# Running block sums of gate and up: kept in one PSUM bank instead of added on VectorE

## The chip, the cores and the metric

The kernel runs on one core of one Trainium2 chip. The metric is the device time of one execution in microseconds (us), of which a median over runs is given. TensorE (PE in the profile) multiplies, with its weight loads listed as PEld; VectorE (DVE), ScalarE (ACT) and GpSimd (POOL) work element by element; SyncE (SP) issues DMAs. Each engine runs its own instructions in order. Products land in PSUM, which has eight banks of 128 x 512 fp32 here; everything else lies in SBUF.

## The reference, cut to what matters

```python
xn = _layernorm(x)                      # x: 2048 x 512
s  = _A_ref(xn, wqkv, w_phi, wo)        # linear attention, 32 heads of 16
gate = xn @ W_gate                      # 512 x 1376
up   = xn @ W_up
h    = gate * (gate > 0) * up           # relu(gate) * up
g    = silu(h @ W_down)                 # 1376 x 512
return x + s * g
```

## The kernel before

**Precision.** Every matmul operand is split into a high part and a remainder, both fp32r. One product is then three matmuls (low x high, high x low, high x high), written by `mm3`; with two tiles of the contraction that is six matmuls of 128 x 128 by 128 x 512. `split` makes the two parts: ScalarE copies the high one (`hh`), GpSimd subtracts for the low one (`hl`).

**Stages.** First come the projections of k, v and q for 16 tiles of 128 tokens, whose state products gather in four PSUM banks, the list `PKV`. Then come two halves. Each handles two blocks of 512 tokens: the gate/up stage over `NF` = 11 blocks of 128 columns of F (f = 0 to 10), with the down-projection of earlier blocks woven in, and then a tail with the rest of the down-projection, the SiLU and the output. The first half also splits all weights for the first time (`f_prep`); the split weights are spilled to memory and reloaded (`f_reload`) later.

**Gate/up by seven products.** For one f, two token blocks times two halves of the contraction, for gate and for up, would be eight block products; seven are formed instead, in the manner of Strassen and Winograd: the inputs A11, A12, A22 and the sums S1 to S4 lie ready in `XT`, and sums of the weights in wa, wb, wc, wd. In `gate_up` (lines 535 to 588) the products are, by the names used below:

| name | bank | input, weight | then, before the change |
|---|---|---|---|
| P1 | pa | A11, wa | ScalarE copies it to t1 (`t<-pa`) |
| P2 | pb | S2, wb | VectorE: m = pb + t1 (`u<-pb,t`) |
| P3 | pc | S3, wb | e7 = pc + m on VectorE (`e<-pc,u`); where `copied`, ScalarE copies pc (`e<-pc`) |
| P4 | pd | S1, wc | VectorE: e7 = pd + e7 (`e<-pd,e`) |
| P5 | pc, onto P3 | A22, wc | VectorE: pc = pc + m (`pc<-pc,u`); where `copied`, GpSimd before it: e7 = e7 + m (`e<-e,u`) |
| P6 | pa, onto P1 | A12, wa | VectorE: e7 = max(pc, 0) * e7, then the split of h1 |
| P7 | pd, onto P4 | S4, wd | VectorE: m = pd + m (`u<-pd,u`), m = max(pa, 0) * m (`u<-pa,u`), the split of h0 put off to the next block (`LATE`, `last_split`) |

`copied` holds in the second half from f = 2. In the profile a tile's name stands without its number, so m is `u`, t1 is `t` and e7 is `e`.

**What else runs meanwhile.** `run` steps `gate_up` from yield to yield. After the third, fifth, sixth and seventh yield it takes one step of the down-projection (`down`, bank `py`) if one is pending; each step covers two blocks of F. Steps become pending after f = 1, 3, 5 and 7, eight at a time, and first read h1 of those two blocks. The sums of the steps are VectorE additions in the first half (`y<-py,y`), and ScalarE copies with GpSimd additions in the second. In between, `pace.pump()` lets a planner, `Clock`, add work of other chains: the queries' softmax (`q_pair`, mostly VectorE), their products (`pnum`), and the weight splits. The planner keeps an estimated time for each engine and adds work only while an engine's estimated backlog is below a limit (`LIMIT`). All instructions stay in program order on their engine.

At f = 10 the pending steps have been drained and the queries finished before `gate_up` begins. In the first half, `used(c)` there reloads input c for the second half as soon as its last product is issued; `halfway` reloads the later weights of f + 1.

Of the kernel before, what the change touches and what calls it, by code (L numbers as in the profile page):

```python
# [8 lines left out]
F32R = mybir.dt.float32r  # L9
AF = mybir.ActivationFunctionType  # L10
ALU = mybir.AluOpType
AX = mybir.AxisListType

P = 128
# [6 lines left out]
NF = -(-F // P)  # L21
BT = 512
TPB = BT // P
NB = S // BT
NG = 8
# [10 lines left out]
A11, A12, A22, S1, S2, S3, S4 = range(7)  # L36
# [112 lines left out]
def layer_kernel(ctx: ExitStack, tc: tile.TileContext, x, wkT, wqT, wv, wo, wf, cst, out):  # L149
# [6 lines left out]
    def ps(shape=(P, 512), name="ps"):  # L156
        return pp.tile(list(shape), F32, tag="ps", name=name)
# [7 lines left out]
    def u2(shape, name, dt=F32):  # L165
        return sb.tile(list(shape), dt, tag="u2", bufs=B2, name=name)
# [10 lines left out]
    def add(engine, o, a, b, op=ALU.add):  # L177
        engine.tensor_tensor(o, a, b, op=op)
# [4 lines left out]
    def split(hi, lo, src, lo_engine=None):  # L183

        nc.scalar.activation(hi, src, AF.Copy)
        add(lo_engine or nc.vector, lo, src, f32(hi), ALU.subtract)

    def mm3(ps_out, w, m, ks, first=True, last=True):

        n = len(ks)  # L190
        for i, k in enumerate(ks):
            (wh, wl), (mh, ml) = w(k), m(k)
            mm(ps_out, wl, mh, first and i == 0, False)
            mm(ps_out, wh, ml, False, False)
            mm(ps_out, wh, mh, False, last and i == n - 1)
            if i < n - 1:
                pace.pump()
# [222 lines left out]
    def kv_products(n):  # L420
        phl, vhl = PHI.pop(n), VH.pop(n)
        if n == 0:
            PKV.extend(ps((P, 2, 256), name="pkv") for _ in range(NG // 2))
        for g in range(NG):
            mm(PKV[g // 2][:, g % 2, :], vhl[:, g, :, :], phl[:, g, :, :],
               n == 0 and g % 2 == 0, n == N - 1 and g % 2 == 1)
# [88 lines left out]
    def f_reload(f, part):  # L515
        if part == 0:
            FT[f] = [w_pair("wa"), w_pair("wb"), None, None]
            for i, t in enumerate([*FT[f][0], *FT[f][1]]):
                nc.sync.dma_start(f32(flat3(t)), wspill[f][i])
            return  # L520
        FT[f][2:] = w_pair("wc"), u2((P, 2, 2, P), "wd", F32R)
        WD[f] = u2((P, D), "fdh", F32R), u2((P, D), "fdl", F32R)
        for i, t in enumerate([*FT[f][2], FT[f][3], *WD[f]]):
            nc.sync.dma_start(f32(flat3(t)), wspill[f][4 + i])

    def w_of(f, i, c=None):
        t = FT[f][i]
        if c is None:
            return lambda k: (t[:, 0, k, :], t[:, 1, k, :])
        return lambda k: (t[0][:, c, k, :], t[1][:, c, k, :])  # L530

    def a_of(c):
        return lambda k: (XT[:, c, 0, k, :], XT[:, c, 1, k, :])

    def gate_up(f, copied, used, halfway):

        pa = ps(name="pa")
        mm3(pa, w_of(f, 0, 0), a_of(A11), range(2))
        used(A11)
        t1 = u2((P, BT), "t1")  # L540
        nc.scalar.activation(t1, pa, AF.Copy)
        last_split()
        yield
        pb = ps(name="pb")
        mm3(pb, w_of(f, 1, 0), a_of(S2), range(2))
        used(S2)
        m = u2((P, BT), "u2")
        add(nc.vector, m, pb, t1)
        yield
        pc = ps(name="pc")  # L550
        mm3(pc, w_of(f, 1, 1), a_of(S3), range(2))
        FT[f][1] = None
        used(S3)
        halfway()
        e7 = u2((P, BT), "e7")
        if copied:
            nc.scalar.activation(e7, pc, AF.Copy)
        else:
            add(nc.vector, e7, pc, m)
        yield  # L560
        pd = ps(name="pd")
        mm3(pd, w_of(f, 2, 0), a_of(S1), range(2))
        used(S1)
        add(nc.vector, e7, pd, e7)
        yield
        mm3(pc, w_of(f, 2, 1), a_of(A22), range(2), first=False)
        FT[f][2] = None
        used(A22)
        if copied:
            add(nc.gpsimd, e7, e7, m)  # L570
        add(nc.vector, pc, pc, m)
        yield
        mm3(pa, w_of(f, 0, 1), a_of(A12), range(2), first=False)
        FT[f][0] = None
        used(A12)
        h1 = u2((P, BT), "hh", F32R), u2((P, BT), "hl", F32R)
        nc.vector.scalar_tensor_tensor(e7, pc, 0.0, e7, op0=ALU.max, op1=ALU.mult)
        split(*h1, e7, nc.gpsimd)
        yield
        mm3(pd, w_of(f, 3), a_of(S4), range(2), first=False)  # L580
        used(S4)
        add(nc.vector, m, pd, m)
        nc.vector.scalar_tensor_tensor(m, pa, 0.0, m, op0=ALU.max, op1=ALU.mult)
        h0 = u2((P, BT), "hh", F32R), u2((P, BT), "hl", F32R)
        LATE.append(lambda: split(*h0, m, nc.gpsimd))
        FT.pop(f)
        HS[f] = [h0, h1]
        yield

    HS, Y, LATE = {}, {}, []  # L590

    def last_split():
        while LATE:
            LATE.pop()()
# [465 lines left out]
    def run(g, per=1):  # L1060
        n = 0
        for _ in g:
            pace.pump()
            n += 1
            if pending and n in (3, 5, 6, 7):
                if next(pending[0], pending) is pending:
                    pending.pop(0)
                    if pending:
                        next(pending[0])
                pace.pump()  # L1070
# [7 lines left out]
    for half in range(2):  # L1078
        b0, b1 = 2 * half, 2 * half + 1
        for f in range(NF):  # L1080
            if half == 0:
                at[0] = N + f
                pace.finish(preps, lambda: f in DONE)
                if f == 0:
                    queries = pace.add(all_queries(0), 20)
            if half == 1 and f == 0:
                queries = pace.add(all_queries(1), 5)
            again = f + 1 < NF and (half or f + 1 in AHEAD)
            if again and f + 1 not in FT:
                f_reload(f + 1, 0)  # L1090
            if f == NF - 1:
                drain()
                pace.finish(queries)
                for q in QUERIES[half][:4]:
                    if q not in OF:
                        o_load(q)
                WO = wo_load()
            if f == NF - 2 and not half:
                for q in QUERIES[half][:2]:
                    o_load(q)  # L1100

            def used(c):
                if half == 0 and f == NF - 1:
                    nc.sync.dma_start(f32(XT[:, c]), xt_spill[:, c])
            run(gate_up(f, half and f > 1, used, lambda: again and f_reload(f + 1, 1)))
            for c, fs in enumerate(CHUNKS[:-1]):
                if f == fs[-1]:
                    pending.extend(down((b0, b1)[j], j, fs, c == 0) for j in (1, 0))

        last_split()  # L1110
        drain()
        if half == 0:
            f_reload(0, 0)
            f_reload(0, 1)
        fs = CHUNKS[-1]
        for j, b in enumerate((b1, b0)):
            j = 1 - j
            if b == b0:
                for q in QUERIES[half][:2]:
                    o_split(q)  # L1120
            parts = {}
            for i in range(TPB):
                if j == 1 and i < 3:
                    parts[i] = ps(name="py")
                    down_rows(parts[i], i, j, fs[:-1], True, False)
            for i in range(TPB):
                if i in parts:
                    down_rows(parts[i], i, j, fs[-1:], False, True)
                else:
                    parts[i] = ps(name="py")  # L1130
                    down_rows(parts[i], i, j, fs, True, True)
                y_sum(b, i, parts[i], False, True)
                y = Y[b][:, i, :]
                nc.scalar.activation(y, y, AF.Silu)
                if b * TPB + i in yspill:
                    pace.when(y, lambda t=b * TPB + i, y=y: nc.sync.dma_start(yspill[t], y))
                pace.pump()
        for g in fs:
            HS.pop(g), WD.pop(g)
        qs = QUERIES[half]  # L1140
        for m, q in enumerate(qs):
            if half == 0 and m == 1:
                f_reload(1, 0)
            if m + 2 < len(qs):
                o_split(qs[m + 2])
            if m + 4 < len(qs):
                o_load(qs[m + 4])
            for j in range(2):
                out_tile(2 * q + j, WO)
                pace.pump()  # L1150
# [56 lines left out]
```

## Time and profile before

| | |
|---|---|
| median of 3 runs | 580.02 us (577.81 to 581.3) |
| span of the profiled execution | 576.0 us |
| own device time of that execution | not listed; the median is 4.0 us above the span |
| TensorE busy | 565.9 us, 98% |
| VectorE, ScalarE, GpSimd busy | 409.0, 280.8, 417.1 us |
| granted TensorE clock | 1.000 |
| first half, f = 0 to 10 | from 175.9 us on |
| second half, f = 0 to 10 | from 368.4 us on |

Rows of the timeline read: start, duration, engine, line, operation, output<-inputs, shapes and count. Matmuls are pipelined, so the recorded durations of neighbours overlap and the spacing of their starts is what counts. A wait row reads: engine and tile, what released it, total us, number, longest. In a group row the count is followed by the busy us and the mean ns of one, and after the second bar by the idle time before them.

### The profile page before, as it was taken

Reading aid. Unit: us, or ns where it says so; the run is one execution under the profiler, and the core shown is the slowest. Engines: PE = TensorE matmul, PEld = TensorE weight load, DVE = VectorE, ACT = ScalarE, POOL = GpSimd, SP = SyncE. Lnnn points to the kernel's source line nnn. Section 1 sums busy time; section 2 is a strip of 40 time slices with the busy share of each in tenths; the row PEclk is TensorE's granted clock in tenths of the full one; section 3 lists DMA queues with packets and bytes.
Section 4 is the critical chain, followed back from the end, with each engine's and each line's share of the span. In section 5 each row is a group of like instructions: output and inputs, shape, how many; then the busy total and the mean of one; then the engine's idle time right before and its main releaser. Section 6 shows DMA issues by size and latency. Waiting matters only on the chain.

```text
span 576.0 us, 8601 instructions
## 1 busy us (share of the span) xinstructions
PE 565.9 (98%) x2848; PEld 479.1 (83%) x2848; DVE 409.0 (71%) x609; ACT 280.8 (49%) x505; POOL 417.1 (72%) x351
## 2 busy tenths in 40 slices
PE   8899999999999999999999999999999999999997
PEld 7788888989898788888888888788888888888886
DVE  3798666768674989699888442599896969874322
ACT  3796876756544536526435133223545444534600
POOL 0669888977879177999798424364759888888475
PEclk9999999999999999999999999999999999999999
DMA  8248899884589927878877999998656766659963
GB/s 315 91 151 225 225 289 273 248 231 95 150 229 283 382 77 262 268 259 273 279 266 259 254 298 424 392 371 302 168 198 201 236 204 191 204 157 318 256 188 111
DMA packets 82523, 138.25 MB, mean 240 GB/s; under 512 B 7600, under 2 KB 30512, under 8 KB 81584
## 3 DMA queue, kind: packets, MB, share of 16 engines
q1 hardware_dynamic: 79024, 125.60, 64.9%
q0 software_dynamic: 3312, 12.06, 11.0%
q8 instruction: 22, 0.36, 0.3%
q14 instruction: 21, 0.17, 0.1%
q10 hardware_dynamic: 144, 0.07, 0.0%
HBM read 77.14 MB, written 52.69 MB: 225 GB/s over the span
## 4 chain that ended last, share of the span: by engine, by line
PE 49%; DVE 2%; POOL 1%; issue 0%; ACT 0%; POOLq 0%; DVEq 0%
PE py L52 16%; PE pso L52 8%; PE pa L52 7%; PE pc L52 7%; PE pd L52 7%; PE pb L52 3%; PE pnum L52 2%; POOL y L52 0%; DVE mx L52 0%; POOL pTl L52 0%; DVE eq L52 0%; DVE e L52 0%; POOL hl L52 0%; DVE pq L52 0%; POOL ez L52 0%
## 5 line engine op out<-in xcount | busy, mean ns | idle before, releaser
L52 PE MATMUL py<-fdh,hl 128*128 128x512 f32 x176 | 68.6, 390 | 0.0
L52 PE MATMUL py<-fdh,hh 128*128 128x512 f32 x176 | 68.5, 389 | 0.0
L52 PE MATMUL py<-fdl,hh 128*128 128x512 f32 x176 | 68.5, 389 | 0.0
L52 PE MATMUL pa<-XT,wa 128*128 128x512 f32 x264 | 67.3, 390 | 0.0
L52 POOL TENSOR_TENSOR hl<-e,hh 128x512 fp32r<-128x512 f32 x22 | 29.1, 1322 | 40.6 <-ACT hh L52 35.7
L52 PEld LDWEIGHTS pa<-XT,wa 128*128 128x128 f32 x264 | 49.3, 188 | 10.1
L52 POOL TENSOR_TENSOR phl<-ek,phl 128x1024 fp32r<-128x1024 f32 x15 | 36.4, 2426 | 24.5 <-ACT phl L52 24.5
L52 ACT ACTIVATE hh<-e 128x512 fp32r<-128x512 f32 x22 | 13.9, 633 | 72.7 <-DVE e L52 67.9
L52 DVE TENSOR_TENSOR y<-py,y 128x512 f32<-128x512 f32 x40 | 27.5, 688 | 29.0 <-PE py L52 29.0
L52 POOL TENSOR_TENSOR hl<-u,hh 128x512 fp32r<-128x512 f32 x22 | 28.6, 1298 | 18.7 <-ACT hh L52 18.5
L52 PEld LDWEIGHTS py<-fdh,hh 128*128 128x128 f32 x176 | 33.0, 188 | 7.0
L52 PEld LDWEIGHTS py<-fdl,hh 128*128 128x128 f32 x176 | 33.1, 188 | 6.9
L52 PEld LDWEIGHTS py<-fdh,hl 128*128 128x128 f32 x176 | 33.0, 188 | 6.8
L52 POOL TENSOR_TENSOR ez<-eq,zB 128x1024 f32<-128x1024 f32 x16 | 38.7, 2426 | 0.0
L52 PE MATMUL pc<-XT,wc 128*128 128x512 f32 x132 | 35.2, 393 | 0.3 <-DVE e L52 0.3
L52 PE MATMUL pq<-XT,wqh 128*128 128x256 f32 x192 | 35.4, 282 | 0.0
L52 POOL TENSOR_TENSOR ol<-of,oh 128x1024 fp32r<-128x1024 f32 x8 | 19.1, 2402 | 21.7 <-ACT oh L52 10.5
L52 PE MATMUL pv<-wvh,XT 128*128 128x512 f32 x96 | 33.2, 400 | 1.0 <-ACT pqs L52 1.0
L52 PE MATMUL pd<-XT,wd 128*128 128x512 f32 x132 | 34.1, 392 | 0.0
L52 PE MATMUL pc<-XT,wb 128*128 128x512 f32 x132 | 33.7, 389 | 0.0
L52 PE MATMUL pd<-XT,wc 128*128 128x512 f32 x132 | 33.7, 389 | 0.0
L52 PE MATMUL pb<-XT,wb 128*128 128x512 f32 x132 | 33.5, 389 | 0.0
(166 smaller groups left out, 1665.6 us busy)
## 6 DMA issues: line engine op xcount, KB each, us to landing
zacc<-ek POOLq DMA_DIRECT2D x15, 512.0 KB, 5.7
xts<-XT SPq DMA_DIRECT2D x4, 1792.0 KB
XT<-xts SPq DMA_DIRECT2D x7, 1024.0 KB, 18.8
wa<-ws SPq DMA_DIRECT2D x26, 256.0 KB, 4.8
wb<-ws SPq DMA_DIRECT2D x26, 256.0 KB, 4.8
wc<-ws SPq DMA_DIRECT2D x26, 256.0 KB, 5.4
rawg<-wf SPq DMA_DIRECT2D x22, 256.0 KB, 3.9
ws<-wa SPq DMA_DIRECT2D x22, 256.0 KB, 4.2
```

Of the source, the lines that this page charges most:

```text
L52: return self.tc.keep_in_program_order(op(*a, **k))
```

## The change

For f = 1 to 10 of both halves the running sums stay in one PSUM bank for the whole stage. It is the fourth bank of `PKV`, named `pseed` now, whose state products have been read by then; it is never given back, so seven banks are left for all other tiles. ScalarE copies P1 into it, and P2, P3 and P5 accumulate onto that copy; ScalarE copies the bank out after P2 (m) and after P3 (e7). The products run in the order P1, P7 of the block before, P2, P6, P3, P4, P5. P7 and what follows it are put off into the next block (`CARRY`, `last_product`), and the split of h1 is put off too (`LATE`). f = 0 keeps its old form in `gate_up_apart`, up to the split of h1 and P7, which are put off as well. Steps of the down-projection still follow the yields 3, 5, 6 and 7, which are now those after P2, P3, P4 and P5. `halfway` is now called after P6.

```diff
@@ kv_products
-            PKV.extend(ps((P, 2, 256), name="pkv") for _ in range(NG // 2))
+            PKV.extend(ps((P, 2, 256), name=s) for s in ("pkv", "pkv", "pkv", "pseed"))
@@ gate_up
-    def gate_up(f, copied, used, halfway):
+    def gate_up(f, used, halfway):
         pa = ps(name="pa")
         mm3(pa, w_of(f, 0, 0), a_of(A11), range(2))
         used(A11)
+        if f == 0:
+            yield from gate_up_apart(f, pa, halfway)
+            return
+        pb = PKV[-1].rearrange("p a f -> p (a f)")
+        nc.scalar.activation(pb, pa, AF.Copy)
+        last_split()
+        yield
+        last_product()
+        yield
+        last_split()
+        mm3(pb, w_of(f, 1, 0), a_of(S2), range(2), first=False)
+        used(S2)
+        m = u2((P, BT), "u2")
+        nc.scalar.activation(m, pb, AF.Copy)
+        yield
+        mm3(pa, w_of(f, 0, 1), a_of(A12), range(2), first=False)
+        FT[f][0] = None
+        used(A12)
+        halfway()
+        yield
+        mm3(pb, w_of(f, 1, 1), a_of(S3), range(2), first=False)
+        FT[f][1] = None
+        used(S3)
+        e7 = u2((P, BT), "e7")
+        nc.scalar.activation(e7, pb, AF.Copy)
+        yield
+        pd = ps(name="pd")
+        mm3(pd, w_of(f, 2, 0), a_of(S1), range(2))
+        used(S1)
+        add(nc.vector, e7, pd, e7)
+        yield
+        mm3(pb, w_of(f, 2, 1), a_of(A22), range(2), first=False)
+        FT[f][2] = None
+        used(A22)
+        finish_f(f, pa, pb, pd, m, e7, used)
+        yield
+
+    def gate_up_apart(f, pa, halfway):
...
-        if copied:
-            nc.scalar.activation(e7, pc, AF.Copy)
-        else:
-            add(nc.vector, e7, pc, m)
+        add(nc.vector, e7, pc, m)
...
-        if copied:
-            add(nc.gpsimd, e7, e7, m)
         add(nc.vector, pc, pc, m)
         yield
         mm3(pa, w_of(f, 0, 1), a_of(A12), range(2), first=False)
         FT[f][0] = None
-        used(A12)
+        finish_f(f, pa, pc, pd, m, e7, lambda c: None)
+        yield
+
+    CARRY = []
+
+    def finish_f(f, gate0, gate1, pd, m, e7, used):
         h1 = u2((P, BT), "hh", F32R), u2((P, BT), "hl", F32R)
-        nc.vector.scalar_tensor_tensor(e7, pc, 0.0, e7, op0=ALU.max, op1=ALU.mult)
-        split(*h1, e7, nc.gpsimd)
-        yield
-        mm3(pd, w_of(f, 3), a_of(S4), range(2), first=False)
...
+        nc.vector.scalar_tensor_tensor(e7, gate1, 0.0, e7, op0=ALU.max, op1=ALU.mult)
+        LATE.append(lambda: split(*h1, e7, nc.gpsimd))
+
+        def last():
+            mm3(pd, w_of(f, 3), a_of(S4), range(2), first=False)
+            used(S4)
+            add(nc.vector, m, pd, m)
+            nc.vector.scalar_tensor_tensor(m, gate0, 0.0, m, op0=ALU.max, op1=ALU.mult)
+            h0 = u2((P, BT), "hh", F32R), u2((P, BT), "hl", F32R)
+            LATE.append(lambda: split(*h0, m, nc.gpsimd))
+            FT.pop(f)
+            HS[f] = [h0, h1]
+        CARRY.append(last)
+
+    def last_product():
+        CARRY.pop()()
@@ the loop over f, and after it
-            def used(c):
-                if half == 0 and f == NF - 1:
+            def used(c, last=half == 0 and f == NF - 1):
+                if last:
                     nc.sync.dma_start(f32(XT[:, c]), xt_spill[:, c])
-            run(gate_up(f, half and f > 1, used, lambda: again and f_reload(f + 1, 1)))
+            def rest():
+                if again:
+                    f_reload(f + 1, 1)
+            if f == 1 and not half:
+                pace.finish(queries, lambda: kvacc is not None)
+            run(gate_up(f, used, rest))
...
+        last_split()
+        last_product()
         last_split()
         drain()
```

More of the change, by code (lines that the diff above doesn't have):

```diff
@@ L539, in gate_up @@
         used(A11)
+        if f == 0:
[35 more added lines that the diff above has]
+    def gate_up_apart(f, pa, halfway):
         t1 = u2((P, BT), "t1")
         nc.scalar.activation(t1, pa, AF.Copy)
-        last_split()
         yield
@@ L545, in gate_up @@
         mm3(pb, w_of(f, 1, 0), a_of(S2), range(2))
-        used(S2)
         m = u2((P, BT), "u2")
@@ L552, in gate_up @@
         FT[f][1] = None
-        used(S3)
         halfway()
         e7 = u2((P, BT), "e7")
-        if copied:
-            nc.scalar.activation(e7, pc, AF.Copy)
-        else:
-            add(nc.vector, e7, pc, m)
+        add(nc.vector, e7, pc, m)
         yield
@@ L562, in gate_up @@
         mm3(pd, w_of(f, 2, 0), a_of(S1), range(2))
-        used(S1)
         add(nc.vector, e7, pd, e7)
@@ L567, in gate_up @@
         FT[f][2] = None
-        used(A22)
-        if copied:
-            add(nc.gpsimd, e7, e7, m)
         add(nc.vector, pc, pc, m)
@@ L574, in gate_up @@
         FT[f][0] = None
-        used(A12)
+        finish_f(f, pa, pc, pd, m, e7, lambda c: None)
+        yield
+    CARRY = []
+    def finish_f(f, gate0, gate1, pd, m, e7, used):
         h1 = u2((P, BT), "hh", F32R), u2((P, BT), "hl", F32R)
-        nc.vector.scalar_tensor_tensor(e7, pc, 0.0, e7, op0=ALU.max, op1=ALU.mult)
-        split(*h1, e7, nc.gpsimd)
-        yield
-        mm3(pd, w_of(f, 3), a_of(S4), range(2), first=False)
[L581 to L588, printed above, removed]
+        nc.vector.scalar_tensor_tensor(e7, gate1, 0.0, e7, op0=ALU.max, op1=ALU.mult)
[12 more added lines that the diff above has]
+        CARRY.pop()()
     HS, Y, LATE = {}, {}, []
```

## The prediction

> **What bounds the kernel now.** I read the page's table of engines first, then the granted clock, then TensorE's own waits.
>
> ```profile
> span 576.0 us, 8601 instructions
> ...
> PE 565.9 (98%) x2848; PEld 479.1 (83%) x2848; DVE 409.0 (71%) x609; ACT 280.8 (49%) x505; POOL 417.1 (72%) x351
> ```
>
> ```profile
> core 0: 576.0 us, clock 1.000
> ```
>
> ```profile
> PE pxT L52 <- DVE lr L52: 2.0, 1, 2.0
> ...
> PE pc L52 <- DVE e L52: 0.3, 1, 0.3
> ```
>
> TensorE is at work in 98% of the span at a full clock, and in the gate/up stages it has one listed wait, of 0.3 us. The change keeps its matmuls, so their time cannot fall; what can move is only how long TensorE stands between them. The timeline gives the spacing, and how fast a reader follows:
>
> ```profile
> 293.86 1.52 PE L52 MATMUL pa<-XT,wa 128*128 128x512 f32 x6
> 295.22 1.52 PE L52 MATMUL pb<-XT,wb 128*128 128x512 f32 x6
> 295.42 0.60 ACT L52 ACTIVATE t<-pa 128x512 f32<-128x512 f32 x1 [4.18 <-PE pa L52]
> 295.91 0.62 ACT L52 ACTIVATE hh<-u 128x512 fp32r<-128x512 f32 x1
> ```
>
> A product of six matmuls takes a turn of 1.36 us (295.22 - 293.86) and is finished 1.52 us after its start; an idle reader starts 0.04 us later. ScalarE starts its next operation 0.49 us after the last. A step of down-projection over two blocks of F is also six 128x512 matmuls, 1.36 us (called D). What a late writer costs is visible where no D stands between two products on one bank:
>
> ```profile
> 372.50 1.52 PE L52 MATMUL pd<-XT,wc 128*128 128x512 f32 x6
> 373.23 0.69 DVE L52 TENSOR_TENSOR e<-pc,u 128x512 f32<-128x512 f32 x1 [0.20 <-DVE u L52]
> 373.98 1.66 PE L52 MATMUL pc<-XT,wc 128*128 128x512 f32 x6
> 375.47 0.84 PE L52 MATMUL pa<-XT,wa 128*128 128x512 f32 x3
> ```
>
> P5 should start at 373.86; VectorE lets the bank go at 373.92, and P6 starts at 375.47, not 375.22. So 0.25 us are lost: a product's turn effectively begins 0.19 us after the release (373.92 + 0.19 - 373.86). I use 0.19 us below. The largest such loss in the stages is this one:
>
> ```profile
> 267.83 1.52 PE L52 MATMUL pd<-XT,wc 128*128 128x512 f32 x6
> 269.61 1.66 PE L52 MATMUL pc<-XT,wc 128*128 128x512 f32 x6 [0.26 <-DVE e L52]
> ```
>
> 269.61 - 269.19 is 0.42 us, with some 0.1 us in the longer 1.66: about 0.5 us. One more of 0.2 us, at f = 1 of the second half, is like the first (an estimate from it). These 0.7 us are all that the change can win back in the blocks it touches; the example at 373 us is in f = 0, which keeps its code.
>
> **The change part by part.** Durations of what is removed and added:
>
> ```profile
> L52 DVE SCALAR_TENSOR_TENSOR u<-pa,u 128x512 f32<-128x512 f32 x22 | 15.2, 692 | 0.8
> L52 DVE TENSOR_TENSOR u<-pd,u 128x512 f32<-128x512 f32 x22 | 15.0, 684 | 3.3 <-PE pd L52 3.3
> L52 ACT ACTIVATE hh<-u 128x512 fp32r<-128x512 f32 x22 | 13.8, 629 | 3.7 <-DVE u L52 3.6
> L52 ACT ACTIVATE t<-pa 128x512 f32<-128x512 f32 x22 | 13.2, 598 | 38.3 <-PE pa L52 37.4 <-POOL y L52 0.8
> L52 POOL TENSOR_TENSOR e<-e,u 128x512 f32<-128x512 f32 x9 | 13.0, 1445 | 6.2 <-DVE e L52 6.2
> ```
>
> **Engine work** is worth nothing by itself. VectorE loses three additions in eleven blocks (f = 1 to 10 of the first half, f = 1 of the second) and two in nine: 51 x 0.69 = 35 us. ScalarE gains two copies in the eleven and one in the nine: 31 x 0.60 = 19 us. GpSimd loses nine additions, 9 x 1.445 = 13 us. All run beside TensorE.
>
> **The new order** is what costs. Today P2 goes to a bank of its own, and only P5 waits on a sum. Afterwards P2, P3 and P5 each write the bank that ScalarE has just written or read, and whatever holds ScalarE holds TensorE, with all matmuls queued behind. I write a product's start as 0 and count.
>
> (a) P1, copy into the bank, P7 of the block before, P2. P1 ends at 1.52, the copy runs from 1.56 to 2.16 (no row shows a ScalarE write to PSUM; I take the 0.598 of `t<-pa`, the other ScalarE copies being near it), plus 0.19 is 2.35; P2's turn is at 2.72. Slack 0.37 us. The row above shows ScalarE in time for 37.4 us of idling; of the 22 copies, three were later than the slack, first and last of them:
>
> ```profile
> 199.58 1.52 PE L52 MATMUL pa<-XT,wa 128*128 128x512 f32 x6
> 201.84 0.58 ACT L52 ACTIVATE t<-pa 128x512 f32<-128x512 f32 x1
> ...
> 403.92 1.53 PE L52 MATMUL pa<-XT,wa 128*128 128x512 f32 x6
> 406.32 0.61 ACT L52 ACTIVATE t<-pa 128x512 f32<-128x512 f32 x1
> ```
>
> 201.84 - 201.10 - 0.04 - 0.37 is 0.33, the last 0.46; the three sum to 1.0 us. For 20 blocks: 0.9 us, from 0 to 2.
>
> (b) P7, then on VectorE `u<-pd,u` and the maximum, then on ScalarE the high half of h0, then the copy of P2, then P3. The copy is queued behind the high half, and this is the longest chain. From P7's start: addition at 1.56, maximum 0.72 later, high half at 3.01, copy 3.50 to 4.10, plus 0.19 is 4.29. P3's turn comes after P2, a D and P6, at 5.44: slack 1.15 us for a late VectorE. How late it is today, at the same addition (seven of 22 over the slack, 5.0 us together) and at `u<-pb,t` a little later in the block (five, 8.0 us), first and last of each:
>
> ```profile
> 227.77 1.52 PE L52 MATMUL pd<-XT,wd 128*128 128x512 f32 x6
> 230.60 0.68 DVE L52 TENSOR_TENSOR u<-pd,u 128x512 f32<-128x512 f32 x1
> ...
> 525.20 1.54 PE L52 MATMUL pd<-XT,wd 128*128 128x512 f32 x6
> 528.18 0.68 DVE L52 TENSOR_TENSOR u<-pd,u 128x512 f32<-128x512 f32 x1
> ```
>
> ```profile
> 263.72 1.54 PE L52 MATMUL pb<-XT,wb 128*128 128x512 f32 x6
> 268.10 0.68 DVE L52 TENSOR_TENSOR u<-pb,t 128x512 f32<-128x512 f32 x1
> ...
> 485.54 1.52 PE L52 MATMUL pb<-XT,wb 128*128 128x512 f32 x6
> 490.63 0.68 DVE L52 TENSOR_TENSOR u<-pb,t 128x512 f32<-128x512 f32 x1
> ```
>
> For 16 such blocks that is 3.6 or 5.8 us; with VectorE freed of the backlog it is 0. I take 3.0, near the lower row, because VectorE has fewer sums but the planner fills it with query work up to its limit. Four blocks (f = 1 and f = 10 of each half) have no D: P3's turn is at 4.08, before 4.29, so each loses 0.21 us with nothing late, 0.8 us in all; with the mean lateness of `u<-pd,u`, 0.82 us in these 22, it would be 4.1. I take 1.5.
>
> (c) The split of h1 is put off until after the next P1, and the first D now follows P2, not P3; in every second block it reads that h1. From P1's start: high half at 2.05, low half on GpSimd at 2.76 to 4.06 (1.30), plus 0.19 is 4.25; the matmuls that read it have their turn at 4.08 + 0.68 = 4.76. Slack 0.51 us for GpSimd's queue, in eight blocks. Of 44 low halves ten start later than that today, by 9.2 us in all, first and last:
>
> ```profile
> 233.12 0.63 ACT L52 ACTIVATE hh<-u 128x512 fp32r<-128x512 f32 x1
> 235.57 1.30 POOL L52 TENSOR_TENSOR hl<-u,hh 128x512 fp32r<-128x512 f32 x1
> ...
> 437.91 0.66 ACT L52 ACTIVATE hh<-u 128x512 fp32r<-128x512 f32 x1
> 439.93 1.32 POOL L52 TENSOR_TENSOR hl<-u,hh 128x512 fp32r<-128x512 f32 x1
> ```
>
> No D reads them so soon today, so it costs nothing. 8 x 9.2 / 44 = 1.7 us, from 0 to 3.4.
>
> (d) The copy into the bank also waits for the previous block's maximum to have read it: P5, D, P1 lie between, so VectorE may be 1.98 us late at P5, and 0.37 more before P2 waits. Its worst is
>
> ```profile
> 426.67 1.52 PE L52 MATMUL pc<-XT,wc 128*128 128x512 f32 x6
> 431.57 0.69 DVE L52 TENSOR_TENSOR pc<-pc,u 128x512 f32<-128x512 f32 x1
> ```
>
> 3.38 us, 1.0 over. With an estimated 0.4 for f = 2 of each half, which lacks that D and has 0.99 us of slack, 1.8 at most; I take 0.7, VectorE being relieved.
>
> P5 after the copy of P3 has P4 and a D or two between, slack 1.7 us and more: nothing. The reloads of wc, wd and the down weights are issued one product and one D later (2.7 us) and land in about 5 us, wanted a block of seven products and four D later (11 x 1.36 = 15 us); without that cover they would cost their landing once. The reload of S4 still follows P7 of the last block, before the tail of the half, whose down-projection and output matmuls hide it as they do today:
>
> ```profile
> wc<-ws SPq DMA_DIRECT2D x26, 256.0 KB, 5.4
> ```
>
> Nothing for these on SP's queue, which they enter in another order (A12 third, not sixth); GpSimd's queue is passed by h1's low half alone, counted in (c).
>
> **The sum:** 0.9 + 3.0 + 1.5 + 1.7 + 0.7 = 7.8 us, less 0.7 won back: +7.1. The span goes from 576.0 to 583.1; the device time of the profiled execution is not listed, and the median of 580.0 is 4.0 above the span, so 587. With every upper bound, 2 + 5.8 + 4.1 + 3.4 + 1.8 - 0.7 = +16.4: 596. With every lower one, +0.1: 580.
>
> **The rivals.** *The slack holds* (not slower). If `u<-pd,u` starts within 1.15 us of its product and the low half of h1 within 0.51 us of its turn, TensorE loses only the 0.8 us of the four blocks and some 0.8 in (c): 580 + 1.6 - 0.7 = 581. For it: most rows are in time, and VectorE is relieved of 35 us. Against it: GpSimd, late in (c), is relieved only in the second half.
>
> *The relief is refilled.* The planner issues query work whenever it believes VectorE free, so the freed 35 us are filled and its queue is as long as now: (b) 5.8, (d) 1.8, hence 587 + 2.8 + 1.1 = 591. The change then does not do what it says: VectorE is not less late where it matters.
>
> *Banks run short.* One bank is bound for good, and pa and pd live on into the next block, four in all at P7. The step sums of D then hold TensorE:
>
> ```profile
> DVE y L52 <- PE py L52: 29.0, 21, 3.3
> ```
>
> VectorE waited for 21 of its sums, so some 19 came late; if each costs its own 0.69 us, +13: 600. Against: TensorE's waits hold none for a sum of D today.
>
> *The clock falls.* Lateness like that in the second pair of rows of (b) means waits of 1.6 and 2.4 us (490.63 - 487.06 - 0.04 - 1.15). If the two products after each took twice as long, 4 x 1.36 = 5.4: 592. After today's wait of 2.0 us the mean clock still reads 1.000. [...]
>
> **How the numbers follow.** Forecast 0.50, slack holds 0.26, refilled 0.14, banks 0.05, clock 0.02, and 0.03 for a gain that I see no source of. About 0.5% (2.9 us) is what can be told from no change here: 0.03 faster, 0.26 same, 0.71 slower. The range goes from 579, below the rival that holds, to 597, over the sum of upper bounds; outside lie the banks and the unseen gain.
>
> **What would show it.** Right: TensorE's waits list ScalarE for `pb` products (a, b), above all in the four blocks without D, and GpSimd's `hl` for `py` (c); matmul counts stay 2848 and VectorE has 51 operations fewer. Wrong: a waits list as empty as before (slack holds), or waits of `py`, `pd` or `pa` on a VectorE sum (banks). A PE busy time over 2 us lower would mean that matmuls themselves got faster, which nothing here allows.

## The result, and the profile after

The changed kernel takes 583.63 us (median of nine runs, 582.29 to 587.15), the kernel before, on the same chip, 579.72 (nine runs, 576.53 to 581.3). The ratio is 1.0084, with an interval of 1.006 to 1.0107: slower by 3.9 us as the medians differ, by 4.9 as the ratio has it, where the prediction said 7.1. The profiled execution took 582.29 us, its span is 4.3 us longer than before, and TensorE's mean granted clock is 1.000 again.

The page's span and table of engines:

```profile
span 580.3 us, 8580 instructions
...
PE 567.5 (98%) x2848; PEld 478.5 (82%) x2848; DVE 377.9 (65%) x558; ACT 297.9 (51%) x536; POOL 407.6 (70%) x342
```

The work moved as forecast: TensorE's matmuls are still 2848, VectorE has 51 operations fewer and is busy 31 us less (35 had been said), ScalarE has 31 more and 17 us more (19), GpSimd nine fewer. None of that is time of the kernel, since TensorE fills 98% of the span as before. What it now waits for, in its list of waits (the first row is the start-up's, as before):

```profile
PE pxT L52 <- DVE lr L52: 2.0, 1, 2.0
...
PE pso L52 <- DMA sx<-x: 1.0, 1, 1.0
PE pv L52 <- ACT pqs L52: 1.0, 2, 0.7
PE pseed L52 <- ACT u L52: 1.0, 2, 0.6
PE py L52 <- POOL hl L52: 0.6, 1, 0.6
PE pseed L52 <- ACT pseed L52: 0.5, 1, 0.5
```

Before, the gate/up stages had one listed wait, of 0.3 us. Now `pseed`, the bank of the sums, waits for ScalarE's copy into it (`ACT pseed`) and for its copy out of it (`ACT u`), and the down-projection for a low half (`POOL hl`). The list leaves out short waits, so I measured the spacing of all matmul starts in the timeline (0.227 us where nothing waits, 0.12 for the query products, whose 256 columns are half as many) and summed what is over. A wait also makes the first spacing behind it some 0.11 us longer (0.34 for 0.227 from 269.46 us on); that is counted in.

| start | block | who waits for whom | lost, us | term |
|---|---|---|---|---|
| 191.1 | f = 1, first half | P2 for the copy of P1 | 0.74 | (a) |
| 220.7 | f = 3, first half | P3 for the copy of P2 | 0.63 | (b) |
| 395.7 | f = 2, second half | P3 for the copy of P2 | 0.87 | (b) |
| 194.6, 331.9, 384.5, 523.8 | f = 1 and 10 of both halves | P3 for the copy of P2 | 0.23, 0.21, 0.21, 0.21 | (b), no D |
| 236.2 | f = 4, first half | D for the low half of h1 | 0.31 | (c) |
| 268.5 | f = 6, first half | D for the low half of h1 | 0.82 | (c) |
| 250.7 | first half | inside a P2 | 0.07 | (a) |
| 546.7 | tail of the second half | first output product | 1.3 | not foreseen |

They sum to 5.6 us. The waits of before that are gone, found in the same way, come to 1.4: 0.53 at 269 us, 0.23 at 383 and 0.08 at 195 in gate/up products, and 0.35 at 443 and 0.17 at 460 where a query product waited for GpSimd's low part (`pTl`). 4.2 us of net loss stand beside 4.3 us of span.

**The copy of P2 behind a late VectorE.** The timeline at 392 us, TensorE, ScalarE and VectorE:

```profile
391.81 1.52 PE L52 MATMUL pseed<-XT,wb 128*128 128x512 f32 x6
...
394.52 1.52 PE L52 MATMUL pa<-XT,wa 128*128 128x512 f32 x6
396.65 1.66 PE L52 MATMUL pseed<-XT,wb 128*128 128x512 f32 x6 [0.60 <-ACT u L52]
```

```profile
395.48 0.63 ACT L52 ACTIVATE hh<-u 128x512 fp32r<-128x512 f32 x1 [3.71 <-DVE u L52]
396.01 0.58 ACT L52 ACTIVATE u<-pseed 128x512 f32<-128x512 f32 x1
```

```profile
392.03 1.18 DVE L52 SCALAR_TENSOR_TENSOR qd<-qs 128x64 f32<-128x64 f32 x1
...
394.04 0.68 DVE L52 TENSOR_TENSOR u<-pd,u 128x512 f32<-128x512 f32 x1
394.75 0.69 DVE L52 SCALAR_TENSOR_TENSOR u<-pa,u 128x512 f32<-128x512 f32 x1
```

Read it from the bottom. P7 has its turn 1.36 us before P2, at 390.45, so its addition could start at 392.01; VectorE is still at query work (`qd`) and starts it at 394.04, 2.03 us late. The high half of h0 (`hh<-u`) follows, and only then ScalarE's copy of P2 out of the bank, although P2 has been finished for 2.7 us (391.81 + 1.52 = 393.33). P3's turn is at 395.88 (394.52 + 1.36); it starts at 396.65. 2.03 less the slack of 1.15 is 0.88; the loss is 0.87. At f = 3 of the first half the addition is 1.78 us late, and the loss 0.63 again fits. In the other 14 blocks with a D it is at most 1.08 us late, inside the slack, and P3 waits in none.

**The low half behind GpSimd's queue.** The timeline at 268 us, TensorE and GpSimd:

```profile
268.52 0.39 PE L52 MATMUL py<-fdh,hh 128*128 128x512 f32 x1
269.46 0.50 PE L52 MATMUL py<-fdh,hl 128*128 128x512 f32 x1 [0.55 <-POOL hl L52]
```

```profile
261.99 4.78 POOL L52 TENSOR_TENSOR ez<-eq,zB 128x1024 f32<-128x1024 f32 x2
266.71 1.45 POOL L52 TENSOR_TENSOR tab<-rawg 128x256 f32<-128x256 f32 x2
268.10 1.30 POOL L52 TENSOR_TENSOR hl<-e,hh 128x512 fp32r<-128x512 f32 x1
```

GpSimd has no idle time before the low half: two query products of 2.4 us each and two sums of weights lie ahead of it, and D stops in its middle, at the first matmul that needs `hl`.

**The copy of P1.** ScalarE at 189 us:

```profile
188.99 2.22 ACT L52 ACTIVATE zB<-pz 32x128 f32<-32x128 f32 x8
191.23 0.58 ACT L52 ACTIVATE pseed<-pa 128x512 f32<-128x512 f32 x1
```

Eight small copies for the queries stand before the first copy into the bank, which ends at 191.81; P2 follows at 191.96, 0.68 us after its turn. In the other 19 blocks the copy is in time, but for the 0.07 us inside a P2 at 250.7.

**The tail.** TensorE, GpSimd and SP's queue at 515 to 548 us:

```profile
546.74 0.39 PE L52 MATMUL py<-fdh,hh 128*128 128x512 f32 x1
548.17 0.50 PE L52 MATMUL pso<-woh,ol 128*128 128x512 f32 x1 [1.05 <-DMA sx<-x]
```

```profile
545.75 7.11 POOL L52 TENSOR_TENSOR ol<-of,oh 128x1024 fp32r<-128x1024 f32 x3 [11.73 <-DMA ol<-eq]
```

```profile
528.41 0.32 SPq L52 DMA_DIRECT2D wol<-wo  x1
529.07 0.52 SPq L52 DMA_DIRECT2D od<-eq  x1
530.40 0.51 SPq L52 DMA_DIRECT2D ol<-eq  x1
533.54 0.51 SPq L52 DMA_DIRECT2D od<-eq  x1
536.81 0.51 SPq L52 DMA_DIRECT2D ol<-eq  x1
```

The wait is credited to `sx<-x`, but the first output product reads `ol`, which GpSimd starts at 545.75 only: it had waited 11.73 us for a store of a query tile (`ol<-eq`) to leave that buffer. Those stores stand in SP's queue behind the loads of the output weights (`wol<-wo`, the last at 528.41), and go out some 3.2 us apart. In the trace of before the same loads go out six to seven us earlier, the last at 522.42, and the eight stores that follow them are issued in two groups of four within 2.5 us each; none holds `ol`.

### The profile page after: what moved, and what is told of

Same layout as the page of the kernel before. It is cut to its first block, busy times and chain, and to the rows that moved or that the text cites. A ratio compares the mean times of both kernels' runs of the same rounds, so it can differ in the third digit from the quotient of the medians.

```text
span 580.3 us, 8580 instructions
## 1 busy us (share of the span) xinstructions
PE 567.5 (98%) x2848; PEld 478.5 (82%) x2848; DVE 377.9 (65%) x558; ACT 297.9 (51%) x536; POOL 407.6 (70%) x342
## 4 chain that ended last, share of the span: by engine, by line
PE 71%; POOL 9%; DMA 9%; issue 4%; DVE 3%; ACT 2%; SPq 0%; POOLq 0%; ACTq 0%; DVEq 0%
PE py L52 16%; PE pseed L52 12%; PE pd L52 8%; PE pa L52 8%; PE pso L52 8%; PE pq L52 5%; PE pv L52 4%; PE pk L52 4%; DMA wol<-wo 3%; PE pnum L52 2%; DMA pql<-pq 2%; POOL phl L52 2%; POOL XT L52 1%; DMA ws<-wd 1%; PE pkv L52 1%
## 5 line engine op out<-in xcount | busy, mean ns | idle before, releaser
L52 PE MATMUL pseed<-XT,wb 128*128 128x512 f32 x240 | 62.0, 393 | 1.4 <-ACT u L52 1.0
L52 PEld LDWEIGHTS pseed<-XT,wb 128*128 128x128 f32 x240 | 44.4, 188 | 13.2 <-ACT u L52 3.3
L52 POOL TENSOR_TENSOR y<-y,ys 128x512 f32<-128x512 f32 x24 | 31.1, 1297 | 9.0 <-ACT ys L52 9.0
L52 DVE TENSOR_TENSOR e<-pd,e 128x512 f32<-128x512 f32 x22 | 15.1, 687 | 27.5 <-PE pd L52 19.6
```

Of the source, the lines that this page charges most:

```text
L52: return self.tc.keep_in_program_order(op(*a, **k))
```

## The experiments

Each run is compared with the kernel before on the same chip. Unless said otherwise, an edit is made to the changed kernel.

**Copy first.** The copy of P2 goes ahead of the high half of h0, so that it waits for nothing but P2.

```diff
-        last_split()
         mm3(pb, w_of(f, 1, 0), a_of(S2), range(2), first=False)
...
         nc.scalar.activation(m, pb, AF.Copy)
+        last_split()
```

> The changed kernel, with ScalarE's two steps after P7 swapped: the copy of the bank after P2 (m) comes before the high half of h0, so the copy no longer stands behind two VectorE operations. Theory A (TensorE loses its time to late readers and writers of the one bank and to the late low half of h1): the six waits at P3, 2.4 us in the profile of the changed kernel (0.23, 0.63, 0.87 and three of 0.21), vanish; TensorE's waits hold no row for pseed behind u; span about 578, time about 581.2. Rival B (the bank that is held for good, or the planner's other order, costs the time): P3's waits may go, but the time stays near 583.6.

581.36 us against 578.14, ratio 1.0048 (1.0029 to 1.0067). Of its waits of TensorE:

```profile
PE py L52 <- POOL hl L52: 2.4, 2, 1.6
```

No wait of `pseed` on `u` is left in any block, those of the four without D included, so (b) is what the chain above says: 2.4 us. But the losses to h1's low half grew from 1.1 to 3.2 us (1.03 at 236 us, 1.89 at 269, 0.29 at 491), though its place in the program is the same. At 269 us the same query products and sums lie ahead of it on GpSimd and run 1.9 us later, where TensorE's step comes 0.75 us later; what shifted them no run here settles. The tail's wait is absent, though the last load of the output weights goes out later still (531.31): four stores stand behind them instead of eight, and none holds `ol`. That the time came out at the expected 581.2 all the same is luck, since neither the growth of (c) nor the end of the tail's wait was expected.

**Split early.** h1 is split where it is made, not in the next block.

```diff
-        LATE.append(lambda: split(*h1, e7, nc.gpsimd))
+        split(*h1, e7, nc.gpsimd)
```

> The changed kernel, with the split of h1 issued at once behind the maximum, as before the change, and not after the next P1. Theory A: the two waits of down-projection steps for GpSimd's low half (0.31 and 0.82 us in the profile) vanish, 1.1 us less, time about 582.5; ScalarE then stands still for a late VectorE before the next P1, which may make the copy into the bank late in a block or two (0 to 0.5 us). Rival B: no change, 583.6.

585.69 us, ratio 1.0125 (1.0102 to 1.0147): slower, not faster. The low half is never late in the gate/up stages now (0.2 us are lost to one in the second half's tail). In its place TensorE waits at P2:

```profile
PE pseed L52 <- ACT pseed L52: 6.1, 8, 1.8
```

The high half of h1 now stands on ScalarE before the copy of P1, and waits there for VectorE's maximum. The longest case, ScalarE in the timeline:

```profile
280.07 0.63 ACT L52 ACTIVATE hh<-e 128x512 fp32r<-128x512 f32 x1 [6.08 <-DVE e L52]
280.61 1.06 ACT L52 ACTIVATE eq<-pnum 128x512 f32<-128x512 f32 x2
281.56 0.72 ACT L52 ACTIVATE wa<-rawg 128x256 fp32r<-128x256 f32 x2
282.18 0.59 ACT L52 ACTIVATE pseed<-pa 128x512 f32<-128x512 f32 x1
```

ScalarE idles 6.08 us at its head instruction; whatever came due behind it goes first, and the copy is last. Putting the split off is what makes (a) cost 0.8 us and not the 8.2 that these waits come to with the slower starts behind them.

**A bank held.** The kernel before, with one of the four state banks kept to the end by a one-column read.

```diff
+    held = small(1, "held", 1)
+    nc.scalar.activation(held, PKV[-1][:, 0, 0:1], AF.Copy)
```

> The kernel before, with its fourth state bank kept to the end of the program (one ScalarE copy of one column at the end reads it), so that seven banks serve the rest, and nothing else changed. Theory A: banks are not short, time as before, 579.7, within 0.5 us of before in the span. Rival B: 582 to 584, with TensorE or VectorE waits for banks.

581.56 us, ratio 1.0049 (1.0029 to 1.0069). Two waits come:

```profile
PE py L52 <- DVE eq L52: 2.1, 2, 1.4
```

A down-projection step finds no free bank until VectorE has read a query's scores. With the slower starts behind them they cost 2.7 us. So a missing bank does cost, with the old seven products on four banks. The changed kernel has no such wait: its one held bank does the work of two.

**New order, own banks.** In 17 of the 20 blocks the new order, but P2 and P3 in banks of their own, and VectorE's sums as before; the copy of P1 to SBUF behind the high half of h0.

```diff
-        mm3(pb, w_of(f, 1, 0), a_of(S2), range(2), first=False)
+        if apart:
+            m = u2((P, BT), "u2")
+            nc.scalar.activation(m, pa, AF.Copy)
+            pb = ps(name="pb")
+        mm3(pb, w_of(f, 1, 0), a_of(S2), range(2), first=apart)
...
+        if apart:
+            add(nc.vector, m, pb, m)
```

> The new order of products without the one bank in 17 of the 20 blocks (all of the first half, f = 4 to 10 of the second): P2 and P3 get banks of their own and the sums are VectorE additions again; f = 1 to 3 of the second half stay as changed. Theory A: in those blocks P2 and P3 wait for nothing; of the profile's waits 0.74, 0.23, 0.63 and two of 0.21 us go (2.0 us), the late low half of h1 stays or grows (VectorE is busier), some P5 waits for a VectorE sum as before the change (0 to 1 us): about 582. If the new order alone cost it: 583.6 or more; if the relief of VectorE is worth much, more than 585.

598.45 us, ratio 1.034 (1.0311 to 1.0369), and it tells nothing of the order:

```profile
PE pa L52 <- ACT u L52: 11.0, 10, 3.2
```

P6 goes onto P1's bank, and now waits for the copy of P1, which I had put behind the late split. A fault of my design; but its waits show the clock (last section).

**Own banks, copy at once.** The same in the first half only, with the copy of P1 straight behind P1; the second half is the changed kernel's.

> The first half in the new order with banks of their own for P2 and P3 and the sums on VectorE, the copy of P1 issued at once after P1; the second half as changed. Unlike the first try of this, P6 has no late reader to wait for. Theory A: in the first half the waits of P2 and P3 go (0.74, 0.23, 0.63 and 0.21 us, 1.8 in all), no TensorE wait for a copy of pa; the late low halves of h1 stay (1.1 us, more if VectorE is late); time about 1.5 us under the changed kernel. If the relief of VectorE matters: as the changed kernel or slower.

583.19 us against 577.73, ratio 1.0095 (1.0061 to 1.0128). The waits of P2 and P3 are gone from the first half. Two others stand there, 1.45 and 1.33 us with their slower starts:

```profile
PE pc L52 <- DVE e L52: 1.2, 1, 1.2
...
PE py L52 <- POOL hl L52: 1.1, 1, 1.1
```

With 30 operations more on VectorE than in the changed kernel, P5 waits for its sum. The first half loses 2.8 us here and 2.9 in the next run, the changed kernel on the same chip: in the new order the relief of VectorE is worth about what the chain through the one bank costs. The kernel before, with the same sums on VectorE in the old order, loses only 0.6 us in its first half. So, by one trace of each, the new order costs some 2 us there even with own banks (the fourth state bank stays held in this run too), and the one bank adds next to nothing to that.

**The changed kernel again**, on the chip of the run above.

> The changed kernel itself once more, as a control on the chip of the runs beside it. Theory A (each loss belongs to a place in the program): the same eleven TensorE waits in the gate/up stages, 4 us together, at the same blocks, ratio to before about 1.008. The twelfth wait, 1.3 us ahead of the first output product of the second half, was foreseen by nobody: if it comes again it belongs to the order of DMAs on SP's queue, if not it was an accident of one execution, and the span is about 579.

582.25 us against 577.73, ratio 1.0076 (1.0047 to 1.0105). In gate/up the waits come in the same blocks with the same sizes, within 0.03 us; the tail's is 1.85 us, under the name that the chain gave it:

```profile
PE pso L52 <- POOL ol L52: 1.6, 1, 1.6
```

**One bank, old order.** The products in the order P1 to P7, accumulating in one bank. P7 and the split of h1 stay in their own block too. This takes the order out and leaves the bank.

> The one bank without the new order: P1 to P7 as before the change, P7 in its own block, but P1 copied into the bank and P2, P3 and P5 accumulated there from f = 1 on. Nothing stands between P1 and P2, or between P2 and P3. Theory A: each of the two waits takes 2.16 + 0.19 - 1.36 = 1.0 us in each of 20 blocks, 40 us: about 619. If what costs is not the chain through ScalarE but the held bank or the put-off work, the time is near 583.

618.08 us against 577.73, ratio 1.0688 (1.0645 to 1.0731).

```profile
PE pkv L52 <- ACT pkv L52: 15.1, 20, 1.4
PE pkv L52 <- ACT u L52: 14.3, 20, 0.8
```

(The bank is called `pkv` here.) P2 and P3 wait in all 20 blocks. The 40 gaps are 0.83 to 0.99 us but for one of 1.53, and sum to 35.8; with 0.08 to 0.11 us behind each that is 40.0, and the kernel is 40.4 us slower. One case on TensorE and ScalarE:

```profile
257.89 1.52 PE L52 MATMUL pa<-XT,wa 128*128 128x512 f32 x6
260.18 1.61 PE L52 MATMUL pkv<-XT,wb 128*128 128x512 f32 x6 [0.76 <-ACT pkv L52]
```

```profile
259.45 0.58 ACT L52 ACTIVATE pkv<-pa 128x512 f32<-128x512 f32 x1 [0.92 <-PE pa L52]
```

The copy runs from 259.45 to 260.03, and P2 starts 0.15 us later, 0.93 after its turn at 259.25 (257.89 + 1.36). So the bank's round trip costs about 1 us a time, and the products put in between hide some 37 of 40 us.

**Low half on VectorE.** "Copy first", with h1's low half on VectorE instead of GpSimd.

```diff
-        LATE.append(lambda: split(*h1, e7, nc.gpsimd))
+        LATE.append(lambda: split(*h1, e7, nc.vector))
```

> The kernel with the copy of the bank issued before the high half of h0, and besides h1's low half made by VectorE (0.69 us, where the sums have left room), not by GpSimd (1.30 us and a queue). Theory A: the waits of the down-projection steps for low halves (3.2 us in the kernel with only the copy first) go; left are 0.75 us at f = 1 of the first half and 0.25 in f = 0 of the second: as fast as the kernel before, within 0.5 us. Rival: VectorE, now in order behind ScalarE's high half, is late for P7's addition, and the waits come back at P3 or at P5: 1.003 to 1.006 of before.

580.75 us, ratio 1.004 (1.0019 to 1.0061), not to be told from "copy first" (1.0048). The expected return to the time of before did not come. The waits for `hl` are gone, others are there:

```profile
PE pseed L52 <- ACT pseed L52: 2.1, 2, 1.6
...
PE pnum L52 <- DVE pTl L52: 0.5, 1, 0.5
PE pd L52 <- DVE e L52: 0.4, 1, 0.4
```

**Output weights sooner.** In the second half their loads are issued before the queries are finished, not after.

```diff
                 drain()
+                if half:
+                    WO = wo_load()
                 pace.finish(queries)
...
-                WO = wo_load()
+                if not half:
+                    WO = wo_load()
```

> The changed kernel, with the loads of the output weights at f = 10 of the second half put on SP's queue ahead of the last queries' stores and loads instead of behind them. The control showed the wait of the first output product again (1.9 us): GpSimd's low half for it waits for stores of query data, and those are issued one by one behind the loads of the output weights. Theory A: the wait is a matter of that order, and goes: 1.3 to 1.9 us less than the changed kernel, 1.005 of before; the waits in the gate/up stages stay. Rival: the traffic itself is the limit, and the wait only changes its name.

589.17 us against 578.22, ratio 1.0195 (1.0171 to 1.022). The tail's wait is gone, and a longer one stands earlier:

```profile
PE py L52 <- POOL hl L52: 6.0, 2, 5.5
```

GpSimd was held 5.38 us at an accumulating DMA of the queries, whose data now came behind the weights, with the low halves of the last block in its queue behind that. Behind this wait TensorE ran at a granted clock of 0.5 until 544.7 us. So the order of these DMAs does bear on the tail's wait, but putting the loads first made another, longer one; whether some other order has none is not shown.

**First D later.** "Copy first", and the first D after P6, not P2.

```diff
-            if pending and n in (3, 5, 6, 7):
+            if pending and n in (4, 5, 6, 7):
```

> The kernel with the copy of the bank first, and the first step of the down-projection taken after P6 instead of after P2 (yields 4 to 7 for 3, 5, 6, 7). The step still stands between P2 and P3, so the copy keeps its slack, and GpSimd's low half of h1 gains 1.36 us. Theory A: of the waits of 1.03, 1.90 and 0.29 us for low halves in the kernel with the copy first, about 0.5 is left; with 0.75 at f = 1 and 0.25 in f = 0, 1.5 us of waits in the gate/up stages: before within 0.3 us, 1.000 to 1.002. Rival: the planner's queue on GpSimd shifts with the step and the waits stay: 1.004.

577.79 us against 578.22, ratio 0.9995 (0.9976 to 1.0014): no difference from the kernel before is left.

```profile
PE py L52 <- POOL hl L52: 0.3, 1, 0.3
```

The losses to low halves fell from 3.2 us in "copy first" to 0.6, and by the ratios the kernel is 3.1 us faster than that one (1.0048 to 0.9995): this is (c), all but taken away. The tail's wait is absent too. The later D alone, with the copy of P2 left behind the high half, has no time: that program deadlocks, so what this edit is worth by itself is not shown.

**Queries sooner.** The edits of "first D later", and the planner may start the first half's queries after 12 of its units of time, not 20, so that the eight small copies have left ScalarE before f = 1.

```diff
-                    queries = pace.add(all_queries(0), 20)
+                    queries = pace.add(all_queries(0), 12)
```

> As the kernel with the later step, and the queries of the first half begun 8 products' columns sooner (12 for 20 in the planner's count, 1.7 us), so that the eight small copies of the state's sums on ScalarE are through when f = 1 copies its first product into the bank. Theory A: the wait of 0.75 us at P2 of f = 1 goes; before within 0.3 us, 0.998 to 1.001. Rival: the planner places all queries anew, and other waits come instead.

578.19 us, ratio 1.0011 (0.9995 to 1.0028), span 575.9 us. The wait at f = 1 is gone; a query product now waits 0.8 us for VectorE at 256 us (1.1 with the slower start), and the time is the same. With TensorE busy in 98% of both spans, no version here beats the kernel before.

## Why the prediction was right, and where its sum was off

The direction and the mechanism stand: TensorE's own work did not change, and the price is what its matmuls wait where a product follows on a bank that ScalarE must first write or read. "One bank, old order" puts the price of one such wait at 0.94 to 1.1 us, "copy first" and "first D later" take (b) and (c) away and with them the loss. The sum was 3.2 us too high by the medians. Term by term, in us:

| term | said | measured | |
|---|---|---|---|
| (a) P2 behind the copy of P1 | 0.9 | 0.8 | one place, f = 1 |
| (b) P3 behind the copy of P2, 16 blocks with D | 3.0 | 1.5 | two blocks of 16 |
| (b) four blocks without D | 1.5 | 0.9 | 0.21 to 0.23 each |
| (c) D behind the low half of h1 | 1.7 | 1.1 | two blocks of eight |
| (d) copy into the bank behind the maximum | 0.7 | 0 | |
| won back | -0.7 | -1.4 | two of the five in a query product |
| tail, not foreseen | 0 | 1.3 | |
| sum | 7.1 | 4.2 | |

Some of the nearness is luck: 1.3 of the 4.2 us are the tail's wait, which the prediction had declared hidden. Its own terms come to 2.9 us.

**(a)** was priced by ScalarE's other copies; the groups of after show the copies themselves, and what ended ScalarE's idle time before them:

```profile
L52 ACT ACTIVATE pseed<-pa 128x512 f32<-128x512 f32 x20 | 11.7, 585 | 33.9 <-PE pa L52 33.9
L52 ACT ACTIVATE u<-pseed 128x512 f32<-128x512 f32 x20 | 11.6, 582 | 0.0
```

585 ns into PSUM, where 598 had been taken; the slack of 0.37 us was exceeded at f = 1, where eight small copies stood ahead.

**(b)** is the term that was mis-sized. The chain and its slack of 1.15 us were right: the case at 392 us comes out within 0.01. Wrong was how late VectorE would be. I took it as late as in the trace of before, less a little, on the ground that the planner would refill it. It did not:

```profile
L52 DVE TENSOR_TENSOR u<-pd,u 128x512 f32<-128x512 f32 x22 | 15.1, 686 | 14.6 <-PE pd L52 14.6
```

VectorE now idles 14.6 us before these additions, waiting for P7, where it idled 3.3: it is mostly early. "Own banks, copy at once" ties this to the relief: with the sums still on VectorE in the same order, the addition passes the slack in four blocks of the first half, by 2.8 us together; in the changed kernel it does so in one, by 0.63. The four blocks without D lost the 0.21 us that follow from the spacing alone, and none of the lateness that I had put on top.

**(c)** came in two of its eight blocks, 1.1 us for 1.7. **(d)** never happened: the group of the copies into the bank shows all of ScalarE's idle time ended by P1, none by VectorE's maximum. What was **won back** is twice what I had counted: the two waits of P5 came to 0.76 us, as said, but I had called them all that there is, and two waits of query products for GpSimd's low part (0.52 us) went as well. GpSimd has nine additions fewer in that half; whether that took them away no run isolates.

**The tail** I had declared hidden "as they do today"; it was the reload of S4 that I looked at, not the stores of the queries. That they come behind the loads of the output weights is shown in both traces of the changed kernel; that a late query is what put them there is argued only. No run here isolates it, and the one that moved the loads only moved the wait.

**The base** of 580.0 stands for before, but the 4.0 us above the span were misread. In all 23 executions of the kernel before that stand beside "copy first" the time lies 1.7 to 1.8 us above the span of the same execution, and 1.8 to 2.1 above it in those of the changed kernel. So the profiled execution of before was some 2.2 us faster than the median (an estimate: 4.0 - 1.8), and the 4.0 set it beside the median. The forecast of the difference does not depend on this.

**The rivals.** *The slack holds* (581) is nearest to what VectorE did, but not to ScalarE at f = 1 and GpSimd in (c); with its 1.6 us the time would be inside what can be told from no change, and it is outside. *The relief is refilled* (591) fell with the row above. *Banks run short* (600) is true of the kernel before with a bank held, at 2.7 us and not 13, and false of the change. *The clock falls* (592) did not happen: no wait in the stages exceeds 1 us and the mean clock is 1.000. Its "twice as long" had no row behind it; in "new order, own banks" six matmuls took 2.87 us instead of 1.53 (1.88 times) after a wait of 2.20 us. And the mean of 1.000 after the wait of 2.0 us in the trace of before does not settle what such a wait costs: after 1.97 us in "copy first" the clock was 0.5 (last section).

## What to carry to other kernels

When a sum moves from an idle adder to a bank that the bottleneck must wait for, price the round trip once (here about 1 us: product's end, copy of 0.585, restart), then ask for each block how much other work stands between, and who is ahead of the copy in its engine's queue: a copy that the bottleneck waits for goes first ("copy first" took 2.4 us of waits away), work that waits for a third engine goes behind it (ahead of the copy it cost 8.2 us in "split early"). A relief of an engine that is not the bottleneck is worth what that engine's lateness costs the bottleneck, here, in the old order, at most the 1.4 us that were won back. Waits that were taken away one by one came back elsewhere in three runs here ("split early" 6.1 us listed, "output weights sooner" 6.0, "low half on VectorE" 2.1); the edits that took (a), (b) and (c) away reached the time of before and no less.

## What the hardware showed that I had not expected

After a wait of 2.20 us TensorE ran at half speed for 3.5 us, after one of 3.23 us for 5.7 us. TensorE's timeline of "new order, own banks", twice, and of "copy first" near its start:

```profile
191.14 1.53 PE L52 MATMUL pb<-XT,wb 128*128 128x512 f32 x6
194.86 2.87 PE L52 MATMUL pa<-XT,wa 128*128 128x512 f32 x6 [2.20 <-ACT u L52]
...
472.51 2.93 PE L52 MATMUL pa<-XT,wa 128*128 128x512 f32 x6 [3.23 <-ACT u L52]
```

```profile
26.12 1.08 PE L52 MATMUL pxT<-ident,xn 128*128 128x128 f32 x4 [1.97 <-DVE lr L52]
```

Six matmuls took 2.87 us instead of 1.53; the starts were 0.427 us apart instead of 0.227, until 198.4 us in the first case and 478.2 in the second, and the granted clock was 0.5. After waits of 1.62 ("copy first") and 1.76 us ("split early") the spacing was 0.227 to 0.23 at once but for the first. About 2 us the length alone does not decide: after the 1.97 us in "copy first" the starts of 128 x 512 matmuls were 0.427 us apart until 29.6 us and the clock 0.5, while after 1.99 us at 25.3 us in the kernel before and 1.98 us at 25.2 in the changed kernel the clock stayed at 1.00. What decides there is not shown. Of the prediction's waits of 1.6 and 2.4 us, by these runs the first leaves its sum alone (no slow stretch followed 1.62 us), and the second might not have (one of 3.5 us followed 2.20 us).

A copy by ScalarE from PSUM to PSUM cost about as much as one to SBUF (585 ns, against 582 for `u<-pseed` in the same trace and 598 for `t<-pa` before).
